# Two MoE blocks behind a sigmoid attention: the layers in pairs, and seven products in the second matrices of all batches

## Chip, core and metric

One core of one Trainium2 chip. The metric is the device time of one launch in microseconds (us), and lower is better.

## What is computed

Four batches of 448 tokens go through a sigmoid attention (12 heads of 64) and then through two blocks of 768 channels:

```python
x = attention(q, k, v)                      # 4 x 448 tokens, 768 channels, fp32
xn = x / rms(x) * rms_g                     # first block, inner width 1536
x = (silu(xn @ w_gate) * (xn @ w_val)) @ w_out
h = x @ w_in                                # second block, inner width 2048
out = (h - tanh(h)) @ w_out2
```

## The kernel before

Channels lie on the 128 partitions, and the 448 tokens of a batch are the columns of a matmul. An fp32 factor is split into a high part (rounded to fp32r) and a low part (the rest), and a product is three matmuls: high by high, high by low, low by high. So three matmuls of 448 columns make a "product" of one 128x128 weight block and one tile of tokens.

Two batches are worked on together: `BATCHES = ((0, 1), (2, 3))`. For a pair of batches a 2x2 block of weights times a 2x2 block of tokens takes eight products, or seven with sums of blocks in Strassen's manner (Winograd's form; `PRODUCTS` names the seven: A11 by B11, S1 by T1 and so on). The sums on the token side (T1 to T4) are made by VectorE in `right_sum`, those on the weight side (S1 to S4) likewise. Names: phase "A" is w_gate and w_val (`"Ag"`, `"Av"`), "B" is w_out, "C" is w_in of the second block, "D" is its w_out.

The work is a list `jobs`. A job of A or C is one pair of output chunks: seven times 3 products, 63 matmuls (`seven_units`, L934). A job of B or D takes four inner chunks into all six output chunks: as a SET with seven products 126 matmuls (`set_units`, L877), as PLAIN blocks with eight 144 (`block`, L959). Before, batches 0, 1 run through all of A, B, C, D first, with B and D in rows of six plain blocks; then batches 2, 3 do the same, with six SETs and one PLAIN set. Partial sums of B and D between groups go to DRAM and come back into PSUM by a copy (`seed`).

Weights arrive as float64 words (768 KB a row of six blocks) and are turned into fp32 by two instructions (`values32`, L350 and a cast). For batches 0, 1 this is done once, and the fp32 values, or for three pairs of C the split parts, are written to DRAM. Batches 2, 3 read them back: A and C by SyncE's queue into two buffers of kind `again`, B and D by GpSimd's queue, three jobs ahead (`fetch`), whence the sums S1 to S4 are made anew. Then each factor is split by a cast and a subtraction (L285, L361).

The order on each engine is not the order in the text. Every step is recorded with `add(engines, ...)` with an estimate of its duration, and `Plan.issue` lists the steps onto engines: it looks up to 500 steps ahead, picks by rank among those that can start soonest, and also chooses between ScalarE and VectorE where a copy or a cast may run on either. All DMAs but GpSimd's stand in one queue on SyncE (SP), in that order.

Buffers that the steps below touch: `xs`, 42 units, hold the seven split token factors of three chunk pairs (7 x 3 x 2), so that one pair of batches' factors of A or C fill them; `again` has two buffers; `raw` has three, after the change two.

Of the kernel before, what the change touches and what calls it, by code (L numbers as in the profile page):

```python
# [21 lines left out]
P = 128  # L22
# [3 lines left out]
GR = {"B": 6, "D": 4}  # L26
SG = 4
SPLIT = [("C", p) for p in range(3)]
# [10 lines left out]
FEED = 80  # L39
WINDOW = 500  # L40
N_UNIT, N_MOE, N_RAW, N_WT, N_CV = 74, 40, 3, 9, 3
BACK = 3
# [5 lines left out]
ORDER_1_OUT = [(k, m) for g in range(0, KF1, GR["B"]) for m in range(KM) for k in range(g, g + GR["B"])]  # L48
ORDER_2 = [(k, m) for m in range(KF2) for k in range(KM)]
ORDER_2_OUT = [(k, m) for g in range(0, KF2, GR["D"]) for m in range(KM) for k in range(g, g + GR["D"])]  # L50
# [168 lines left out]
def tile_sigmoid_attention_moe_moe(  # L219
# [81 lines left out]
    PLAIN_FROM = {"B": KF1 - SG, "D": KF2}  # L301
    PG = {ph: KM * n // NB for ph, n in GR.items()}
    PAIRS = {"Ag": (w_gate, "A"), "Av": (w_val, "A"), "C": (w_in2, "C")}
    SECOND = {"B": (w_out, ORDER_1_OUT), "D": (w_out2, ORDER_2_OUT)}


    for bs in BATCHES:
        for names, ph, n, ahead in (
            ([(ph, p) for p in range(KF1 // 2) for ph in ("Ag", "Av")], "B", KF1 // (SG if bs == BATCHES[1] else GR["B"]), int(bs == BATCHES[1])),
            ([("C", p) for p in range(KF2 // 2)], "D", KF2 // (SG if bs == BATCHES[1] else GR["D"]), 1),  # L310
        ):
            per, at = len(names) // n, 0
            for g in range(n):
                to = min((g + 1) * per + ahead, len(names))
                jobs += [(x, bs, p, None) for x, p in names[at:to]]
                if bs == BATCHES[1]:
                    jobs.append((ph, bs, g, SET if g * SG < PLAIN_FROM[ph] else PLAIN))
                else:
                    jobs += [(ph, bs, i, SECOND[ph][1][i * NB:(i + 1) * NB]) for i in range(g * PG[ph], (g + 1) * PG[ph])]
                at = to  # L320
    half = [j for j in range(len(jobs)) if jobs[j][1] == BATCHES[1]][0]


    raws, whls, got, ops = {}, {}, {}, {}
# [861 lines left out]
```

## Time and profile before

| what | us |
|---|---|
| median of 3 runs | 1094.83 (1094.33 to 1095.99) |
| the profiled execution | 1093.64 |
| its span, first to last instruction | 1091.5 |
| TensorE matmuls busy | 1073.5 |
| TensorE weight loads busy | 895.5 |
| VectorE busy | 766.8 |
| ScalarE busy | 574.6 |
| GpSimd busy | 59.6 |

An engine's busy time is the union of its instructions' spans. Matmuls are pipelined and one lasts longer (367 ns) than the step from one to the next, so the step is read from counts in a stretch. The profile is of one execution; the runs' median lies 1.2 us above it.

### The profile page before, as it was taken

How to read it: one execution, taken by the hardware profiler on the slowest of the kernel's cores; microseconds unless marked ns; L12 is line 12 of the kernel's file. 1: busy time of each engine (PE TensorE's matmuls, PEld its weight loads, DVE VectorE, ACT ScalarE, POOL GpSimd, SP SyncE). 2: the span in 40 equal slices, each digit the busy share in tenths (PEclk: the TensorE clock that was granted, in tenths of full speed). 3: DMA queues.
4: the chain of work that ended last, by engine and by line, in shares of the span. 5: the costliest groups of instructions: out<-in, count | busy, mean ns of one | idle time of the engine just before them, and what ended most of it. 6: DMA issues, size and time to landing. Idle time of an engine off the chain costs nothing. (4 is left out here: it accounts for less than half of the span.)

```text
span 1091.5 us, 14829 instructions
## 1 busy us (share of the span) xinstructions
PE 1073.5 (98%) x5256; PEld 895.5 (82%) x5256; DVE 766.8 (70%) x1217; ACT 574.6 (53%) x1036; POOL 59.6 (5%) x76
## 2 busy tenths in 40 slices
PE   9999999999999999999999999999999999999998
PEld 3333338999999998899998889999999889998997
DVE  0453816888488879878786887858855578786877
ACT  5776864552255556446464643444444556565652
POOL 0000000000000000000010000010040000113130
PEclk9999999999999999999999999999999999999999
DMA  5773553588748928699999654353495344538383
GB/s 167 255 218 112 143 180 129 203 260 283 226 162 281 330 112 313 203 315 309 313 345 317 226 185 121 113 200 102 107 224 187 118 147 140 192 86 189 57 207 126
DMA packets 115241, 215.73 MB, mean 198 GB/s; under 512 B 26720, under 2 KB 80992, under 8 KB 115168
## 3 DMA queue, kind: packets, MB, share of 16 engines
q1 hardware_dynamic: 106544, 195.36, 54.4%
q0 software_dynamic: 8320, 19.27, 8.0%
q8 instruction: 41, 0.67, 0.3%
q14 instruction: 32, 0.26, 0.1%
q10 hardware_dynamic: 304, 0.16, 0.0%
HBM read 135.71 MB, written 79.04 MB: 197 GB/s over the span
## 5 line engine op out<-in xcount | busy, mean ns | idle before, releaser
L934 PE MATMUL ps<-unit,wt 128*128 128x448 f32 x2520 | 523.4, 367 | 8.2 <-ACT unit L285 5.1
L934 PEld LDWEIGHTS ps<-unit,wt 128*128 128x128 f32 x2520 | 473.2, 188 | 53.1 <-ACT unit L285 8.4
L285 ACT COPY unit<-ps 128x448 f32<-128x448 f32 x220 | 115.9, 533 | 244.8 <-PE ps L934 91.9
L959 PE MATMUL ps<-unit,wt 128*128 128x448 f32 x1152 | 237.9, 366 | 1.8 <-ACT unit L285 1.8
L959 PEld LDWEIGHTS ps<-unit,wt 128*128 128x128 f32 x1152 | 216.2, 188 | 21.1 <-ACT unit L285 2.1
L361 DVE TENSOR_TENSOR wt<-cv,wt 128x768 fp32r<-128x768 f32 (+1 forms) x188 | 163.5, 876 | 20.9 <-ACT wt L285 17.8
L877 PE MATMUL ps<-unit,wt 128*128 128x448 f32 x756 | 158.0, 367 | 2.5 <-DVE unit L680 1.3
L877 PEld LDWEIGHTS ps<-unit,wt 128*128 128x128 f32 x756 | 141.3, 188 | 16.4 <-DVE unit L806 2.3
L285 ACT CAST wt<-cv 128x768 fp32r<-128x768 f32 (+1 forms) x136 | 104.5, 774 | 89.1 <-PE ps L934 40.4
L680 DVE TENSOR_TENSOR unit<-unit 128x448 fp32r<-128x448 f32 x168 | 102.4, 621 | 18.8 <-ACT unit L285 15.8
L285 ACT CAST unit<-unit 128x448 fp32r<-128x448 f32 x162 | 90.0, 567 | 35.1 <-DVE unit L789 14.4
L806 DVE TENSOR_TENSOR unit<-ps,unit 128x448 f32<-128x448 f32 x132 | 81.4, 621 | 28.3 <-PE ps L934 14.8
L582 ACT ACTIVATE unit<-ps 128x448 f32<-128x448 f32 (+1 forms) x192 | 86.4, 548 | 5.1 <-PE ps L575 5.1
L575 PE MATMUL ps<-wt 64*128 64x448 f32 (+1 forms) x384 | 78.9, 548 | 0.0
L605 PE MATMUL ps<-unit,vs 128*64 128x448 f32 (+1 forms) x384 | 77.7, 546 | 0.0
L350 DVE SCALAR_TENSOR_TENSOR cv<-wt,zero 128x768 uint32<-128x768 uint32 x68 | 64.8, 953 | 7.4 <-ACT zero L285 4.4
L575 PEld LDWEIGHTS ps<-wt 64*128 64x128 f32 (+1 forms) x384 | 32.3, 173 | 43.2 <-issue 36.2
L685 DVE TENSOR_TENSOR unit<-unit 128x448 f32<-128x448 f32 x96 | 59.1, 620 | 10.0 <-ACT unit L285 7.0
L605 PEld LDWEIGHTS ps<-unit,vs 128*64 128x64 f32 (+1 forms) x384 | 25.3, 136 | 49.0 <-issue 32.9
L285 ACT CAST zero<-wt 128x768 f16<-128x768 bf16 x48 | 51.8, 1079 | 20.3 <-DVE cv L350 13.2
L627 DVE TENSOR_TENSOR unit<-unit 128x448 f32<-128x448 f32 x20 | 12.5, 624 | 66.6 <-ACT unit L620 66.5
L419 DVE TENSOR_TENSOR cv<-cv 128x384 f32<-128x384 f32 x80 | 43.2, 554 | 19.2 <-DMA wC<-cv 10.8
(51 smaller groups left out, 523.2 us busy)
## 6 DMA issues: line engine op xcount, KB each, us to landing
wt<-in_w_out SPq DMA_DIRECT2D x28, 768.0 KB, 6.5
wt<-in_w_in SPq DMA_DIRECT2D x16, 768.0 KB, 6.9
sumD<-unit SPq DMA_DIRECT2D x48, 224.0 KB, 4.4
unit<-sumD SPq DMA_DIRECT2D x48, 224.0 KB, 5.3
wt<-in_w_gate SPq DMA_DIRECT2D x12, 768.0 KB, 5.4
wt<-in_w_val SPq DMA_DIRECT2D x12, 768.0 KB, 5.3
wAg<-cv SPq DMA_DIRECT2D x24, 384.0 KB, 4.6
wAv<-cv SPq DMA_DIRECT2D x24, 384.0 KB, 4.5
```

The source lines that it names most:

```text
L285: add(engines, lambda e: (nc.scalar.copy if e == "ACT" else nc.vector.tensor_copy)(to(), of()), reads, writes)
L350: add(dve(NW, psum=False), lambda e: nc.vector.scalar_tensor_tensor(out=c.tile.bitcast(U32), in0=r.tile[:, :NW, 1], scalar=13, in1=z.tile, ...
L361: add({**dve(n, psum=False), **pool(n)}, lambda e: ENG[e].tensor_sub(lo(), of(), hi().bitcast(F32)), [*reads, *kh], [*kl])
L575: nc.tensor.matmul(ps[i, c].tile[:n, :S], lhsT=t.tile[rows, at:at + n], rhs=t.tile[rows, :S], start=True, stop=True)
L582: add(act(S, psum=True), lambda e: nc.scalar.activation(to.tile[at:at + n, :S], ps.tile[:n, :S], AF.Sigmoid, bias=-math.log(S), scale=1.0 ...
L605: nc.tensor.matmul(ps.tile[i * D:(i + 1) * D, :S], lhsT=v.tile[:n, c, i, :], rhs=a[c][i].tile[:n, :], start=(c == 0), stop=(c == 3))
L680: add({**pool(S), **dve(S, psum=False)}, lambda e: ENG[e].tensor_sub(t["l"].tile, of.tile, t["h"].tile.bitcast(F32)), [of["t"], kh], [kl])
L685: add({**dve(S, psum=False), **pool(S)}, lambda e: ENG[e].tensor_sub(t.tile, x.tile, y.tile), [x["t"], y["t"]], [t["t"]])
L806: add(dve(S), lambda e: nc.vector.tensor_add(t.tile, ps.tile[:, :S], t.tile), [ps["t"], t["t"]], [t["t"]])
L877: nc.tensor.matmul(ps.tile[:, :S], lhsT=part(a), rhs=x[b].tile, start=n in (1, 5) and kp == 0 and q == 0, stop=kp == n_kp - 1 and q == 2, ...
L934: nc.tensor.matmul(ps.tile[:, :S], lhsT=part(a), rhs=x[b].tile, start=n in ((1, 2, 5) if opening else (1, 5)) and i == 0 and q == 0, stop= ...
L959: nc.tensor.matmul(ps.tile[:, :S], lhsT=wt, rhs=a[p].tile, start=start and i == 0, stop=stop and i == 2, skip_group_check=True)
```

## The change

Jobs are ordered by pairs of layers. A and B run for batches 0, 1, then for 2, 3; then C and D for batches 0, 1, then for 2, 3. B and D of batches 0, 1 use SETs too: both first B sets and all four D sets; the third B set is PLAIN for both pairs of batches. The rows of w_out and w_out2 are loaded, turned into fp32 and summed to S1 to S4 once, ahead of their use (`rows_early`): those of w_out beside the attention of batches 0 and 1, those of w_out2 beside A of batches 2, 3. All seven factors are written to DRAM. Every SET of every pair of batches reads its seven factors back one by one through SyncE's queue and the two `again` buffers (`again`). B's sums of all batches go to DRAM, by a write for the first set and an adding DMA on GpSimd's queue for the others, and C reads them back (`reload_sum`), with the token factors of C made beside the last job of the layer pair ahead. The three pairs of C whose split parts were stored store fp32 values now. In the two MoE blocks all copies and casts go to ScalarE.

```diff
-SPLIT = [("C", p) for p in range(3)]
+SPLIT = []
+ACT_COPIES = "AgAvBCD"
+PLAIN_SETS = {("B", 0): (2,), ("D", 0): (), ("B", 1): (2,), ("D", 1): ()}
...
-N_UNIT, N_MOE, N_RAW, N_WT, N_CV = 74, 40, 3, 9, 3
+N_UNIT, N_MOE, N_RAW, N_WT, N_CV = 74, 40, 2, 8, 5
...
-    for bs in BATCHES:
-        for names, ph, n, ahead in (
...
+    for names, ph in (
+        ([(x, p) for p in range(KF1 // 2) for x in ("Ag", "Av")], "B"),
+        ([("C", p) for p in range(KF2 // 2)], "D"),
+    ):
+        for bs in BATCHES:
...
+                jobs.append((ph, bs, g, PLAIN if is_plain(ph, bs, g) else SET))
...
+        return [lambda: get("A21", "A22"), lambda: of("A21"), lambda: of("A22"), lambda: total("S1", "A21", "A22", None, sub=False),
+                lambda: get("A11", "A12"), lambda: of("A11"), lambda: total("S3", "A11", "A21", "A21"),
+                lambda: total("S2", "S1", "A11", "S1"), lambda: of("A12"), lambda: total("S4", "A12", "S2", None)]
...
+    def again(d, at):
+        w = slot("again", cv_p, [P, NW], F32, "cv")
+        add({"SP": (1100, False)}, lambda e: nc.sync.dma_start(out=w.tile, in_=d.tile[:, at]), [d[at]], [w[0], w[1]], after=2500)
+        return w
...
+        def one(n):
+            w = again(whole_w[ph, i], ROWS.index(n))
+            whole((j, n), lambda: w.tile, [w[0], w[1]])
...
+    def reload_sum(b, c):
+        x = xg[b, c] = unit("xr")
+        d = sums_t.pop(("B", b, c))
+        add({"SP": (650, False)}, lambda e: nc.sync.dma_start(out=x.tile, in_=d.tile), [d["t"]], [x["t"]], after=2000)
...
-    PHASES = (1, 2, 5, 6, 7, 3, 4)
+    PHASES = {False: (1, 2, 5, 6, 3, 7, 4), True: (1, 5, 6, 3, 7, 2, 4)}
...
-    mixed(attn_units(0))
-    mixed(attn_units(1), [lambda: norm(0), lambda: spread_norm(0)])
+    rows_b = [u for i in range(n_sets("B")) for u in rows_early("B", i)]
+    mixed(attn_units(0), rows_b[:8])
+    mixed(attn_units(1), [lambda: norm(0), lambda: spread_norm(0)], rows_b[8:])
...
-        (last_c, half, [lambda: [spread_norm(b) for b in BATCHES[1]], *x_units(BATCHES[1], True)]),
+        (last["Av", BATCHES[0]], first["Ag", BATCHES[1]], [lambda: [spread_norm(b) for b in BATCHES[1]], *x_units("A", BATCHES[1], True)], BEHIND),
+        (last["Av", BATCHES[1]], first["C", BATCHES[0]], x_units("C", BATCHES[0], True), BEHIND),
+        (last["C", BATCHES[0]], first["C", BATCHES[1]], x_units("C", BATCHES[1], True), BEHIND),
+        (first["Ag", BATCHES[1]], first["C", BATCHES[0]] - 5, [u for i in range(n_sets("D")) for u in rows_early("D", i)], ROWS_BEHIND),
```

On TensorE, behind the attention, before: A of batches 0, 1 (L934) and the rows of w_out (L959), up to the start of C.

```order
L934 MATMUL ps<-unit,wt 128x448 x291
L959 MATMUL ps<-unit,wt 128x448 x6
L934 MATMUL ps<-unit,wt 128x448 x18
L959 MATMUL ps<-unit,wt 128x448 x210
L934 MATMUL ps<-unit,wt 128x448 x360
L959 MATMUL ps<-unit,wt 128x448 x6
L934 MATMUL ps<-unit,wt 128x448 x18
L959 MATMUL ps<-unit,wt 128x448 x210
```

The same place after: L937 are A's products, L880 those of a SET, L962 plain blocks, L661 the spread of the norm of batches 2, 3.

```order
L937 MATMUL ps<-unit,wt 128x448 x234
L880 MATMUL ps<-unit,wt 128x448 x9
L937 MATMUL ps<-unit,wt 128x448 x9
L880 MATMUL ps<-unit,wt 128x448 x108
L937 MATMUL ps<-unit,wt 128x448 x9
L880 MATMUL ps<-unit,wt 128x448 x9
L937 MATMUL ps<-unit,wt 128x448 x171
L962 MATMUL ps<-unit,wt 128x448 x24
L661 MATMUL ps<-unit,ones 128x448
L937 MATMUL ps<-unit,wt 128x448 x3
```

Two groups of 216 plain matmuls (6 and 210 in a row) have become two SETs of 126, of which the second is shown, and one PLAIN set of 144, whose first 24 stand at the end.

On SP, in the first third of the attention, before: loads of q, k (in_qkt) and v (in_vp), and between them the first weights of A.

```order
L536 DMA wt<-in_qkt 128x832
L541 DMA wt<-in_qkt 64x64 x2
L340 DMA wt<-in_w_gate 128x3072
L546 DMA vs<-in_vp 128x384
L546 DMA vs<-in_vp 32x128
L546 DMA vs<-in_vp 64x64 x2
L536 DMA wt<-in_qkt 128x832
L541 DMA wt<-in_qkt 64x64 x2
L340 DMA wt<-in_w_gate 128x3072
```

The same place after: the rows of w_out, and the first stores of their fp32 values (wB).

```order
L536 DMA wt<-in_qkt 128x832
L541 DMA wt<-in_qkt 64x64 x2
L336 DMA wt<-in_w_out 128x3072
L546 DMA vs<-in_vp 128x384
L546 DMA vs<-in_vp 32x128
L546 DMA vs<-in_vp 64x64 x2
L336 DMA wt<-in_w_out 128x3072
L536 DMA wt<-in_qkt 128x832
L541 DMA wt<-in_qkt 64x64 x2
L546 DMA vs<-in_vp 128x384
```

Up to the loads of attention pair 18 of 24 the queue held 5 weight loads and 9 stores of weights before; now it holds 12 loads and 18 stores.

On TensorE at the end of C and D of batches 0, 1, before: the last C job, the last group of rows of w_out2, then A of batches 2, 3.

```order
L934 MATMUL ps<-unit,wt 128x448 x6
L661 MATMUL ps<-unit,ones 128x448 x2
L934 MATMUL ps<-unit,wt 128x448 x39
L959 MATMUL ps<-unit,wt 128x448 x6
L934 MATMUL ps<-unit,wt 128x448 x18
L959 MATMUL ps<-unit,wt 128x448 x138
L934 MATMUL ps<-unit,wt 128x448 x297
```

The end of C and D of batches 0, 1 after: the last C job, the last D set, then C of batches 2, 3.

```order
L937 MATMUL ps<-unit,wt 128x448 x45
L880 MATMUL ps<-unit,wt 128x448 x9
L937 MATMUL ps<-unit,wt 128x448 x9
L880 MATMUL ps<-unit,wt 128x448 x108
L937 MATMUL ps<-unit,wt 128x448 x9
L880 MATMUL ps<-unit,wt 128x448 x9
L937 MATMUL ps<-unit,wt 128x448 x171
```

The 144 plain matmuls between the two layers have become 126, and what follows is another pair of batches in the same layer.

## Rows read from the trace of the kernel before

**Rows 1.** The page, engines' busy time, share of the span, instructions.
```profile
PE 1073.5 (98%) x5256; PEld 895.5 (82%) x5256; DVE 766.8 (70%) x1217; ACT 574.6 (53%) x1036; POOL 59.6 (5%) x76
```

**Rows 2.** Busy time by stretches: length, engines' us (x instructions), PEclk, DMA share, GB/s.
```profile
0.00:50.00 50.00, 48.06 (x236) 18.84 (x238) 10.96 (x16) 33.31 (x73) 1.60 (x8) 1.00 0.67 202
50.00:100.00 50.00, 50.00 (x256) 19.35 (x252) 21.01 (x37) 34.09 (x73) 1.04 (x1) 1.00 0.63 190
...
300.00:350.00 50.00, 50.00 (x247) 46.08 (x246) 41.82 (x66) 25.49 (x40) 0.00 (x0) 1.00 0.66 226
...
400.00:450.00 50.00, 46.74 (x226) 41.68 (x225) 43.76 (x72) 28.26 (x47) 0.00 (x0) 1.00 0.74 262
...
600.00:650.00 50.00, 47.05 (x219) 42.03 (x219) 42.75 (x75) 27.53 (x53) 0.00 (x0) 0.97 0.66 220
...
700.00:750.00 50.00, 50.00 (x248) 46.11 (x247) 34.66 (x52) 20.29 (x35) 3.03 (x4) 1.00 0.50 158
...
850.00:900.00 50.00, 46.68 (x226) 41.76 (x226) 33.93 (x56) 29.32 (x59) 1.51 (x2) 1.00 0.42 139
...
1050.00:1091.50 41.50, 36.62 (x178) 32.82 (x177) 28.01 (x44) 12.25 (x22) 0.91 (x2) 0.99 0.48 145
```

**Rows 3.** TensorE's waits over the whole span: us in total, times, longest.
```profile
PE ps L934 <- ACT unit L285: 5.1, 4, 2.2
PE ps L934 <- DVE unit L806: 2.6, 2, 1.3
PE ps L292 <- POOL mark L1030: 1.9, 1, 1.9
PE ps L959 <- ACT unit L285: 1.8, 1, 1.8
PE ps L877 <- DVE unit L680: 1.3, 1, 1.3
PE ps L877 <- DVE unit L806: 1.2, 1, 1.2
PE ps L934 <- ACT ps L285: 0.2, 1, 0.2
```

**Rows 4.** Groups by form: busy us, mean ns of one, idle before, releasers.
```profile
L934 PE MATMUL ps<-unit,wt 128*128 128x448 f32 x2520 | 523.4, 367 | 8.2 <-ACT unit L285 5.1 <-DVE unit L806 2.6 <-ACT ps L285 0.2
...
L361 DVE TENSOR_TENSOR wt<-cv,wt 128x768 fp32r<-128x768 f32 x151 | 143.6, 955 | 18.1 <-ACT wt L285 15.7
L680 DVE TENSOR_TENSOR unit<-unit 128x448 fp32r<-128x448 f32 x168 | 102.4, 621 | 18.8 <-ACT unit L285 15.8 <-DMA sumD<-unit 0.6
L285 ACT CAST wt<-cv 128x768 fp32r<-128x768 f32 x110 | 91.7, 835 | 78.0 <-PE ps L934 32.0 <-DVE cv L350 21.8 <-DVE cv L419 9.2
...
L350 DVE SCALAR_TENSOR_TENSOR cv<-wt,zero 128x768 uint32<-128x768 uint32 x68 | 64.8, 953 | 7.4 <-ACT zero L285 4.4 <-DMA wAg<-cv 1.4 <-DMA wC<-cv 0.8
L685 DVE TENSOR_TENSOR unit<-unit 128x448 f32<-128x448 f32 x96 | 59.1, 620 | 10.0 <-ACT unit L285 7.0 <-DMA sumD<-unit 2.4
...
L419 DVE TENSOR_TENSOR cv<-cv 128x384 f32<-128x384 f32 x80 | 43.2, 554 | 19.2 <-DMA wC<-cv 10.8 <-DMA wAg<-cv 7.3
...
L361 DVE TENSOR_TENSOR wt<-cv,wt 128x384 fp32r<-128x384 f32 x37 | 20.6, 556 | 2.7 <-ACT wt L285 2.1
```

**Rows 5.** Short stretches at the first and second seam (columns as in Rows 2).
```profile
435.00:440.00 5.00, 3.71 (x19) 3.09 (x18) 4.90 (x10) 1.96 (x5) 0.00 (x0) 1.00 1.04 341
...
605.00:610.00 5.00, 4.42 (x14) 3.97 (x15) 4.80 (x9) 5.00 (x11) 0.00 (x0) 0.66 1.05 381
```

**Rows 6.** TensorE in order of time: start, us, instructions, idle before and releaser.
```profile
605.58 5.50 PE L934 MATMUL ps<-unit,wt 128*128 128x448 f32 x18 [2.18 <-ACT unit L285]
```

**Rows 7.** DMA issues: count, KB each, median us to landing.
```profile
wt<-in_w_in SPq DMA_DIRECT2D x16, 768.0 KB, 6.9
...
cv<-wAg SPq DMA_DIRECT2D x24, 384.0 KB, 3.3
...
wt<-wD POOLq DMA_DIRECT2D x16, 384.0 KB, 6.0
```

More of the change, by code (lines that the diff above doesn't have):

```diff
@@ L499, in tile_sigmoid_attention_moe_moe @@
+    def set_factors(j):
+        ph, _, i, kind = jobs[j]
+        def one(n):
+            w = again(whole_w[ph, i], ROWS.index(n))
+            whole((j, n), lambda: w.tile, [w[0], w[1]])
+        names, n = (("A11", "A12", "A21", "A22"), 2) if kind == PLAIN else ([PRODUCTS[x][0] for x in PHASES[is_tight(j) > 0]], 4)
+        units = [lambda n=n: one(n) for n in names]
+        later[j] = units[n:]
+        return units[:n]
     later = {}
@@ L514, in again_units, with two @@
             return [lambda at=at, names=names: load_parts(at, names) for at, names in enumerate(FACTORS)]
-        g = got.pop(j)
-        def two(t, names):
+        def two(at, names):
+            t = again(stored[ph, i], at)
             of = lambda: t.tile
@@ L807, in plus, with chunks_of @@
         return t
-    n_sets = lambda ph: {"B": KF1, "D": KF2}[ph] // SG
-    PHASES = (1, 2, 5, 6, 7, 3, 4)
+    def chunks_of(j):
+        i = jobs[j][2]
+        return range(i * SG // 2, (i + 1) * SG // 2) if jobs[j][3] else ()
+    PHASES = {False: (1, 2, 5, 6, 3, 7, 4), True: (1, 5, 6, 3, 7, 2, 4)}
+    is_tight = lambda j: next((x for x in (1, 2) if jobs[j][3] and jobs[j - x][3] is None
+                               and jobs[j - x][1] == jobs[j][1] and jobs[j - x][2] in chunks_of(j)), 0)
     def set_units(j, tight):
         ph, bs, s, _ = jobs[j]
-        last = s == n_sets(ph) - 1
+        last = carried(ph, bs, s)
         n_kp = SG // 2
+        late = tight > 0
         banks, accs, f = {}, {}, {}
@@ L946, in seven_units @@
             order = [(n, i) for n in (1, 5, 6, 2) for i in range(3)]
[L947 removed]
+        order += [(n, i) for n in (3, 7, 4) for i in range(3)]
         return [lambda n=n, i=i: product(n, i) for n, i in order]
@@ L999, in job_units @@
             return plain_units(j)
-        def one(n, k, m):
-            w = whls[j]
-            first, last = k % GR[ph] == 0, k % GR[ph] == GR[ph] - 1
-            if first:
-                prologue(ph, bs, m, k // GR[ph])
-            block(bs, ph, k, m, w, n, first and k < GR[ph], last)
-            if last:
-                for b in bs:
-                    epilogue(ph, bs, b, m, k // GR[ph])
-        return [lambda n=n, k=k, m=m: one(n, k, m) for n, (k, m) in enumerate(blocks)]
     pairs = [(b, p) for b in range(B) for p in range(HP)]
@@ L1089, in tile_sigmoid_attention_moe_moe @@
     held = []
[L1090 to L1093 removed]
     for j in range(len(jobs)):
[L1096 to L1098 removed]
         ahead = conv(j + AHEAD) + [lambda: load(j + 2 * AHEAD)]
[L1100 removed]
+        plan.act_copies = jobs[j][0] in ACT_COPIES
         kind = kind_of(j)
[L1102 removed]
+        tight = is_tight(j)
         units = job_units(j, tight)
[L1104 to L1106 removed]
+        cut = {None: 3, SET: 3 if tight else 2, PLAIN: 4}[kind]
         order = units[:cut] + held + units[cut:]
         held = []
[L1109 to L1111 removed]
+        n = 2 if kind == PLAIN else HELD
+        order, held = order[:-n], order[-n:]
         for n, u in enumerate(order):
             u()
[L1114 removed]
+            for j0, j1, more, behind in beside:
                 if j0 <= j < j1:
```

302 lines of the change are left out of this document (128 added, 174 removed).

## The prediction, on record before the changed kernel ran

> **What bounds the kernel now.** I read the page's busy times first: TensorE has work for 98% of the span, VectorE for 70%, ScalarE for 53% [rows 1]. A busy TensorE need not be one at its best pace, so next comes the table by stretches. An undisturbed 50 us hold 247 or 248 matmuls [rows 2], which is 50 / 248 = 0.2016 us from one to the next; the 367 ns that one lasts [rows 4] is pipelined and no price. Three stretches hold fewer: 226, 219 and 226 [rows 2]. The list of TensorE's waits says why: 14.1 us in all, of which 1.9 is the start, the others on copies by ScalarE and additions by VectorE [rows 3]. Those three stretches are seams, where one layer's results become the next layer's token factors. Together they lack 22 + 29 + 22 = 73 matmuls, 73 x 0.2016 = 14.7 us. So the bound is the number of matmuls at 0.2016 us, plus what the seams lose, plus small waits inside the sets (1.3 and 1.2 us, L877 [rows 3]) and the end.
>
> At the first seam VectorE is the one that is late: busy 4.90 of 5 us while TensorE gets 19 matmuls instead of 25 [rows 5]. At the second there is a wait of 2.18 us, and the 18 matmuls behind it take 5.50 us [rows 6] instead of 18 x 0.2016 = 3.6; the granted clock of that stretch is 0.66 [rows 5], so a part of it ran at the lower of TensorE's two levels, 1.2 instead of 2.4 GHz. That wait cost its own length and 1.9 us more.
>
> **The matmuls.** Six groups of plain blocks (two of B, four of D, batches 0, 1, counted in sets of four inner chunks) become SETs: 144 - 126 = 18 matmuls fewer each, 108 in all. A, C, the attention and the third B set keep theirs. At 0.2016 us that is 21.8 us, and nothing hides it, since TensorE is what everything waits for. The Trainium skill ("TensorE: Matmul & The Clock Gate", section "Wait — 56ns, not 53.3ns?") puts a warm stream at columns / 2.4 GHz plus some 2.5 ns, an estimated 0.189 us for 448 columns; by that the term would be 20.4 us. The counts of this trace give 0.2016, with a weight load before each matmul, and they decide.
>
> **The seams.** Before, the last group of B had to be finished before C of the same batches could begin, and that of D before the units of batches 2, 3. Now each seam has another pair of batches in between, so the sums are long done and come back from DRAM; the DMAs (12 of 224 KB at each seam) are not late, as a whole set stands before them. What stays is the work to make the token factors. The `xs` buffers hold one layer's factors, so new ones start only as the last A or C job uses up the old ones. A seam needs 12 sums and 21 low parts on VectorE, 33 x 0.62 us [rows 4] = 20.5 us. At the start of C for batches 0, 1 there is also: two conversions of C pairs, each 2 x 0.953 + 4 x 0.554 + 3 x 0.955 + 0.556 = 7.5 us [rows 4], so 15.1; four splits of the PLAIN set, 3.8; and ten outputs of the last job at 0.62, 6.2. That is 45.6 us. Groups overlap a little at their ends, and the forms of the page add to 5% more than VectorE's 766.8 us, so I count 43.3. TensorE has 63 + 144 = 207 matmuls for it, 41.7 us. VectorE is thus full, not badly overfull. For the C(0, 1) to C(2, 3) seam the sum is 20.5 + 7 (conversions are reloads) + 8.7 (set) + 10.5 (last job's outputs and factors) = 46.7, some 44 against 189 x 0.2016 = 38.1, but a third of the new factors is wanted only inside the first job, 12.7 us later. The A seam is as the C(0, 1) one. A seam can cost nothing (the first products want only two of three chunk pairs) or as much as the worst of before, 29 x 0.2016 = 5.8 us; I take 2.3 each, 7 in all, nearer to the lower end as no chain through the last sums is left. Bounds 0 and 18. So the seams give back 14.7 - 7 = 7.7 us.
>
> **The sets.** Twelve SETs instead of six. The two waits inside sets came to 2.5 us for six, so 2.5 more for six further ones. Those of D for batches 0, 1 stand in the densest stretch: per two C jobs and one set (252 matmuls, 50.8 us) VectorE has two conversions 15.1, the outputs of the jobs 7.5, their token factors 22 x 0.62 = 13.6, seven splits 6.7 and six additions 3.7, together 46.6, by the same 5% 44.3 of 50.8, or 87%. Before, a stretch at 41.82 of 50 ran without a wait [rows 2], and one at 43.76 had the first seam. I add 1.5 us for that, so 4 in all; bounds 0 and 12. ScalarE takes over casts and copies: by the order's counts some 70 more casts of 768 columns at 835 ns [rows 4], 58 us, and about 140 more of 448 columns, estimated at two thirds of that, 80 us. That lifts it from 53% to some 66%. It stays behind VectorE, which rises by only some 20 us by the same counts, since it gives up most of its casts and copies.
>
> **The attention.** The queue takes 7 more weight loads and 9 more stores by pair 18, as the order shows: 7 x 0.786 + 9 x 0.393 = 9.0 MB. At 341 GB/s, which the queues reached at share 1.04 [rows 5], this is 26 us of full DMA within about 100 us, whose share was 0.67 and 0.63 [rows 2]. It becomes about 0.92: full, but the q, k, v loads stand up to three pairs (some 19 us) ahead. VectorE is free there, 10.96 and 21.01 us of 50 [rows 2], and takes most of the conversions. I take 1 us; bounds 0 and 8.
>
> **The sum**, against the profiled execution: 1093.64 - 21.8 - 7.7 + 4 + 1 = 1069.1. The runs' median lies 1.2 us above that execution, so 1070.3; I say 1070.
>
> **The rivals.**
> *Free seams*: 14.7 us come back whole, the sets cost 2.5. 1093.64 - 21.8 - 14.7 + 2.5 + 1.2 = 1060.8. For it speaks that the sums are ready a set ahead; against it the 43 us of VectorE in 42.
> *VectorE becomes the bound* in C and D of batches 0, 1 and at the seams: it decides when VectorE gets no more than the 42 of 50 us that it had in the fullest quiet stretch [rows 2]. Then 44.3 us per cycle take 52.7, 1.9 too many, four times 8; and the seams cost as before. 1093.64 - 21.8 + 8 + 4 + 1.2 = 1085.0. Against it: 4.90 of 5 was reached where it was pressed [rows 5].
> *The clock*: each seam leaves a wait like that of 2.18 us, with 1.9 us at the lower clock behind it, so 3 x 4.1 = 12 in place of 7: 1075. This lies inside the forecast's range. The Trainium skill ("TensorE: Matmul & The Clock Gate", section "What's actually happening") says that activity releases the throttle and idleness brings it back. The trace agrees in one place of seven, granted clock 0.66.
> *The reload loop* (slower): every SET's factor now passes through two `again` buffers: DMA, cast 0.835, subtraction 0.955 [rows 4]. TensorE uses one factor per 18 matmuls, 3.63 us. With the 3.3 us that such a load took [rows 7] a buffer turns in 5.1, and two give one factor every 2.55 us. At the 6.9 us of the w_in loads [rows 7] it is (6.9 + 1.79) / 2 = 4.35, 0.72 too slow, times 84 factors = 60 us: 1093.64 - 21.8 + 60 + 1.2 = 1133. It eats the gain from 6.0 us on, which is what the old set loads took on GpSimd's queue [rows 7]. Against it: A of batches 2, 3 made four such reloads per 12.7 us, one in 3.2 us, and held 248 matmuls per 50 us [rows 2].
> *The attention starves*: DMA full for 75 us, q and k come late by more than their lead. Price up to 10 us: 1080.
>
> **How the numbers follow.** Forecast 0.60 (1063 to 1079), free seams 0.17, VectorE 0.13, starved attention 0.05, reload loop 0.05. The range takes the free seams with some room, and VectorE as the bound: 1058 to 1087. About 0.2%, 2.2 us, is what a measurement of this kernel can tell from no change. Only the reload loop, and the tail of VectorE's case, end above 1092.6: faster 0.94, same 0.02, slower 0.04.
>
> **What would show it.** TensorE's three lines of products must count 2520, 1512 and 288, and an undisturbed 50 us must still hold 247 or 248. The seams should show waits of TensorE on VectorE or ScalarE of 1 to 3 us, the first 150 us none. If free seams are right, no stretch of 50 us falls below 240. If VectorE binds, it is over 45 of 50 us through D of batches 0, 1, with TensorE short in each of its four cycles. If the reload loop binds, ScalarE's casts in the sets wait for DMAs from the stored factors, and these land after 5 us or more. I am wrong in kind if the pace of matmuls changes, or if the three seams lose more than before.

## The result, and the profile after

The changed kernel takes 1102.44 us (median of 4 runs, 1100.51 to 1102.72) where the kernel before took 1094.58 beside it: a ratio of 1.0069, 95% interval 1.005 to 1.0087. It is slower by 0.7%; the forecast was 1070 us, in a range up to 1087. The profiled execution has a span of 1098.7 us (1091.5 before).

The page of the changed kernel, busy times, and the two large DMA queues (packets, MB, share of 16 engines' time):

```profile
PE 1058.4 (96%) x5148; PEld 878.0 (80%) x5148; DVE 770.1 (70%) x1207; ACT 706.7 (64%) x1268; POOL 99.9 (9%) x120
...
q1 hardware_dynamic: 92368, 215.02, 58.9%
q0 software_dynamic: 15552, 24.78, 14.1%
```

The same two queues in the kernel before:

```profile
q1 hardware_dynamic: 106544, 195.36, 54.4%
q0 software_dynamic: 8320, 19.27, 8.0%
```

TensorE has its 108 matmuls fewer than in [rows 1], and is busy for less of the span. Queue 0 is GpSimd's. After, it carries the adding DMAs (adds, for short) and nothing else: 108 of 224 KB are the 24.78 MB. Its share is 0.141 x 1098.7 = 155 us of all 16 engines, **1.43 us for each add**. Before there were 36 adds, and 28 loads of 384 KB.

The stretches that answer to [rows 2] (length, busy us and instructions of PE, PEld, DVE, ACT, POOL, granted clock, DMA share, GB/s):

```profile
50.00:100.00 50.00, 48.79 (x247) 18.93 (x249) 21.89 (x33) 36.35 (x79) 1.03 (x1) 1.00 0.89 291
...
300.00:350.00 50.00, 50.00 (x247) 46.05 (x246) 35.52 (x61) 31.52 (x54) 10.62 (x12) 1.00 0.84 217
...
400.00:450.00 50.00, 45.23 (x220) 40.88 (x220) 37.03 (x57) 28.00 (x49) 4.91 (x6) 1.00 0.86 255
...
600.00:650.00 50.00, 46.97 (x219) 41.99 (x220) 36.45 (x58) 29.66 (x52) 5.26 (x6) 0.97 0.54 157
...
700.00:750.00 50.00, 48.95 (x240) 44.50 (x239) 45.01 (x71) 39.95 (x68) 0.00 (x0) 1.00 0.78 266
750.00:800.00 50.00, 45.11 (x213) 41.11 (x211) 36.52 (x58) 31.55 (x56) 10.38 (x12) 0.94 0.75 194
800.00:850.00 50.00, 43.83 (x215) 40.19 (x213) 33.52 (x54) 29.44 (x55) 10.47 (x12) 0.98 0.67 170
850.00:900.00 50.00, 46.49 (x211) 41.33 (x212) 42.41 (x71) 36.00 (x69) 10.36 (x12) 0.95 0.79 200
...
1000.00:1050.00 50.00, 50.00 (x249) 46.29 (x248) 35.15 (x55) 32.97 (x60) 9.60 (x12) 1.00 0.70 167
```

A quiet stretch still holds 247 to 249 matmuls, so the pace is that of before. But more stretches are not quiet, above all the three from 750 to 900 us (D of batches 0, 1, and the seam behind it). In them GpSimd issues 12 adds each, and in the first two VectorE is far from full. In the last row shown, and in that from 300 us, there are 12 adds too and nothing is lost in the row itself: the adds alone are not enough. (Batches 2, 3, in the last row, convert no weights; that this is what spares them is not shown.)

A balance of the span needs the pace. A stretch counts the matmuls that are under way at its edges, so counts of short stretches are a little high; from start to start the step is 0.2033 us (650 to 850 us of the kernel before). By their starts, the first 200 us hold 970 matmuls (before 989), 3.9 us lost. From 200 us on the other 4178 should take 849.4 of 898.7 us, so 49.3 us are lost with the end; before, 4267 should take 867.5 of 891.5, so 24.0. Hence 1091.5 - 22.0 + 3.9 + 25.3 = 1098.7: the matmuls came off as counted, and 25 us more than before went in waits behind 200 us.

TensorE's two largest waits (in total, times, longest), against 5.1 and 2.6 us in [rows 3]:

```profile
PE ps L937 <- ACT unit L289: 12.2, 4, 6.3
PE ps L937 <- DVE unit L816: 10.0, 5, 4.9
```

The longest, in order of time (start, us, engine, line, and in brackets the idle time before and who ended it):

```profile
829.69 1.76 POOL L754 DMA_DIRECT2D out<-unit  x2 [1.01 <-DVE unit L816]
...
833.24 0.53 ACT L289 COPY unit<-ps 128x448 f32<-128x448 f32 x1 [4.65 <-DMA out<-unit]
...
840.69 0.32 SPq L677 DMA_DIRECT2D unit<-sumB  x1
...
848.81 0.83 ACT L289 CAST wt<-cv 128x768 fp32r<-128x768 f32 x1 [4.30 <-DMA cv<-wC]
...
850.13 6.20 PE L937 MATMUL ps<-unit,wt 128*128 128x448 f32 x18 [6.29 <-ACT unit L289]
```

The chain that led there (start, us, what):

```profile
829.69 8.79 DMA out<-unit
...
840.20 0.88 DVE wt L370
...
841.11 7.68 DMA cv<-wC
```

Read both upwards. TensorE waits 6.29 us for ScalarE, which stands at a cast whose fp32 weights (`cv<-wC`) come 7.7 us after their issue. That load was issued late: the buffer that it fills was in use until VectorE's subtraction (L370) ended at 841.08, and ahead of it in SP's queue the read of a sum (L677) stood until 840.69. VectorE was late itself, by the chain, because an add issued at 829.69 held a unit until it landed after 8.79 us; and ScalarE had stood still for 4.65 us already, for the same reason. Adds land after 8 us (DMA issues: count, KB, median us to landing):

```profile
sumB<-unit POOLq DMA_DIRECT2D x48, 224.0 KB, 8.4
out<-unit POOLq DMA_DIRECT2D x36, 224.0 KB, 8.0
...
cv<-wD SPq DMA_DIRECT2D x56, 384.0 KB, 3.9
```

In stretches of 5 us the DMA engines are full there, and the clock is low behind the wait:

```profile
840.00:845.00 5.00, 3.83 (x19) 3.21 (x18) 3.88 (x6) 2.10 (x4) 1.73 (x2) 1.00 1.11 244
845.00:850.00 5.00, 0.00 (x0) 0.00 (x0) 0.50 (x2) 1.19 (x3) 0.00 (x0) 0.83 1.11 281
850.00:855.00 5.00, 4.87 (x13) 4.35 (x14) 3.49 (x5) 3.97 (x8) 0.00 (x0) 0.50 0.95 355
```

A granted clock of 0.50 is the lower level, 1.2 GHz: 18 matmuls took 6.20 us instead of some 3.7 (18 x 0.2033).

Theory, then: **the 72 additional adds fill the DMA engines in dense stretches**, loads and stores come late, and the engines that work in order pass it on to TensorE. Rivals: the adds hurt by their landing time alone (held units); the reloads of all SET factors are what is too much; the seven products or the order cost it.

### The profile page after: what moved, and what is told of

Same layout as the page of the kernel before. It is cut to its first block, busy times and chain, and to the rows that moved or that the text cites. A ratio compares the mean times of both kernels' runs of the same rounds, so it can differ in the third digit from the quotient of the medians.

```text
span 1098.7 us, 15000 instructions
## 1 busy us (share of the span) xinstructions
PE 1058.4 (96%) x5148; PEld 878.0 (80%) x5148; DVE 770.1 (70%) x1207; ACT 706.7 (64%) x1268; POOL 99.9 (9%) x120
## 3 DMA queue, kind: packets, MB, share of 16 engines
q0 software_dynamic: 15552, 24.78, 14.1%
## 4 chain that ended last, share of the span: by engine, by line
PE 58%; issue 11%; DMA 8%; DVE 4%; ACT 2%; POOL 2%; POOLq 0%; SPq 0%; DVEq 0%; ACTq 0%
PE ps L937 35%; PE ps L880 20%; PE ps L962 3%; DMA out<-unit 1%; POOL out L754 1%; DVE wt L370 1%; DMA cv<-wB 1%; DMA cv<-wAv 1%; DMA unit<-sumB 1%; DMA wt<-in_w_out 1%; ACT wt L289 1%; DMA cv<-wC 1%; DVE unit L685 1%; DMA wt<-in_w_gate 1%; DVE unit L816 1%
## 5 line engine op out<-in xcount | busy, mean ns | idle before, releaser
L937 PE MATMUL ps<-unit,wt 128*128 128x448 f32 x2520 | 530.0, 369 | 22.9 <-ACT unit L289 12.2
L937 PEld LDWEIGHTS ps<-unit,wt 128*128 128x128 f32 x2520 | 476.9, 190 | 69.1 <-ACT unit L289 14.5
L880 PE MATMUL ps<-unit,wt 128*128 128x448 f32 x1512 | 316.3, 366 | 7.3 <-ACT wt L289 3.4
L880 PEld LDWEIGHTS ps<-unit,wt 128*128 128x128 f32 x1512 | 283.0, 188 | 35.0 <-ACT wt L289 4.8
L370 DVE TENSOR_TENSOR wt<-cv,wt 128x768 fp32r<-128x768 f32 (+1 forms) x252 | 223.0, 891 | 113.4 <-ACT wt L289 112.1
L289 ACT CAST wt<-cv 128x768 fp32r<-128x768 f32 (+1 forms) x248 | 193.4, 785 | 92.4 <-DVE cv L359 22.3
L289 ACT COPY unit<-ps 128x448 f32<-128x448 f32 x298 | 156.8, 533 | 116.8 <-PE ps L937 40.8
L685 DVE TENSOR_TENSOR unit<-unit 128x448 fp32r<-128x448 f32 x252 | 152.6, 620 | 28.5 <-ACT unit L289 22.1
L289 ACT CAST unit<-unit 128x448 fp32r<-128x448 f32 x258 | 142.1, 567 | 38.9 <-DVE unit L690 17.7
L816 DVE TENSOR_TENSOR unit<-ps,unit 128x448 f32<-128x448 f32 x168 | 103.8, 621 | 30.2 <-PE ps L937 14.6
L690 DVE TENSOR_TENSOR unit<-unit 128x448 f32<-128x448 f32 x144 | 87.5, 620 | 19.8 <-DMA unit<-sumB 16.4
L754 POOL DMA_DIRECT2D sumB<-unit x48 | 42.1, 990 | 438.5 <-DMA cv<-wB 157.1
L605 PEld LDWEIGHTS ps<-unit,vs 128*64 128x64 f32 (+1 forms) x384 | 25.3, 136 | 50.5 <-issue 32.1
L962 PE MATMUL ps<-unit,wt 128*128 128x448 f32 x288 | 61.1, 368 | 1.8 <-DVE unit L740 1.0
L962 PEld LDWEIGHTS ps<-unit,wt 128*128 128x128 f32 x288 | 53.5, 188 | 8.4 <-DVE unit L740 1.8
```

Source lines behind the costliest of these rows:

```text
L289: add(engines, lambda e: (nc.scalar.copy if e == "ACT" else nc.vector.tensor_copy)(to(), of()), reads, writes)
L370: add({**dve(n, psum=False), **pool(n)}, lambda e: ENG[e].tensor_sub(lo(), of(), hi().bitcast(F32)), [*reads, *kh], [*kl])
L605: nc.tensor.matmul(ps.tile[i * D:(i + 1) * D, :S], lhsT=v.tile[:n, c, i, :], rhs=a[c][i].tile[:n, :], start=(c == 0), stop=(c == 3))
L685: add({**pool(S), **dve(S, psum=False)}, lambda e: ENG[e].tensor_sub(t["l"].tile, of.tile, t["h"].tile.bitcast(F32)), [of["t"], kh], [kl])
L690: add({**dve(S, psum=False), **pool(S)}, lambda e: ENG[e].tensor_sub(t.tile, x.tile, y.tile), [x["t"], y["t"]], [t["t"]])
L816: add(dve(S), lambda e: nc.vector.tensor_add(t.tile, ps.tile[:, :S], t.tile), [ps["t"], t["t"]], [t["t"]])
```

## Experiments: which part of the change

**The order alone.** B and D of batches 0, 1 plain, all else as after.

```diff
-PLAIN_SETS = {("B", 0): (2,), ("D", 0): (), ...
+PLAIN_SETS = {("B", 0): (0, 1, 2), ("D", 0): (0, 1, 2, 3), ...
```

> The changed kernel with plain sets (eight products) in w_out and w_out2 of batches 0, 1; the new order of layers, the rows made ahead, the reloads and the adding DMAs stay. 108 matmuls more, 21.8 us at 0.2016 us. If what the changed kernel loses hangs on the seven products of batches 0, 1 (their token factors and seven reloads instead of four), the losses of 350 to 600 and 700 to 900 us mostly go, some 25 us, and the run ends near 1098. If it hangs on the new order, the sums through adding DMAs and the seams, the run ends at 1115 or more.

Measured 1115.86 us (ratio to before 1.0214, 1.0182 to 1.0245). The seven products are worth 1115.86 - 1102.44 = 13.4 us; order, reloads and adds without them cost 21. So most of the loss is not in the products; of the 22.0 us that 108 matmuls are worth, 8.6 did not come back under the adds.

**No additions in the DMAs.** The adds become plain writes.

```diff
-nc.gpsimd.dma_start(out=d.tile, in_=t.tile, accum_op=ALU.add)
+nc.gpsimd.dma_start(out=d.tile, in_=t.tile)
```

> The adding DMAs on GpSimd's queue become plain writes of the same tiles on the same queue; the additions are left out, so the sums hold only the last part. Theory of the adding DMAs (they land after 8 us, hold the units that ScalarE's next copies and SP's next loads need, and take the DMA engines from the others): 1075 to 1085, and ScalarE's waits on them in the D sets of batches 0, 1 are gone. Theory of the reloads (factors come late through two buffers) or of VectorE's load: within 5 us of the changed kernel's 1102.

Measured 1076.51 us (ratio 0.9851, 0.9829 to 0.9873): 25.9 us come back (24 by the ratios, as the kernel before was 1 us faster beside this run), and the time lies inside the forecast's range. Its queue 0, a row of its DMA issues, and the three stretches that had lost most (as above):

```profile
q0 software_dynamic: 6912, 24.78, 5.7%
...
out<-unit POOLq DMA_DIRECT2D x36, 224.0 KB, 3.0
...
750.00:800.00 50.00, 50.00 (x247) 46.06 (x246) 41.13 (x66) 35.81 (x63) 6.47 (x12) 1.00 0.57 200
800.00:850.00 50.00, 47.54 (x231) 42.59 (x230) 39.27 (x64) 36.20 (x67) 8.28 (x16) 1.00 0.72 242
850.00:900.00 50.00, 47.76 (x226) 43.20 (x225) 42.61 (x70) 33.45 (x62) 4.67 (x9) 0.97 0.46 145
```

The same bytes take 0.057 x 1073.2 / 108 = 0.57 us each instead of 1.43, and those of this row land after 3.0 instead of 8.0 us (those of B after 5.3 instead of 8.4).

**No reloads.** The factors of B and D are split from one fixed tile; 92 reloads of 384 KB are left out.

```diff
-            w = again(whole_w[ph, i], ROWS.index(n))
-            whole((j, n), lambda: w.tile, [w[0], w[1]])
+            whole((j, n), lambda: fixed, [])
```

> The factors of all sets of w_out and w_out2 are split from one fixed tile instead of being read back from DRAM: 92 loads of 384 KB are left out, the casts and subtractions stay. Theory of the reloads: 1075 to 1085, and casts no longer wait for these loads. Theory of the adding DMAs: 1095 or more, as ScalarE still stands behind results whose units are held.

Measured 1088.68 us (0.9954, 0.9939 to 0.9969): 13.8 us back. And both edits together:

> Plain writes for the adding DMAs and a fixed tile for the reloads of the sets together (additions and 92 loads left out). If the two costs are apart: 26 and 14 us off 1102, near 1063. If they are the same cost seen twice (a DMA system that is too full): 1072 to 1076, hardly below plain writes alone. Either way what is left over the number of matmuls is the work of VectorE and ScalarE at the seams and the attention.

Measured 1075.26 us (0.9838, 0.9823 to 0.9853), 1.2 us under the plain writes alone, with overlapping intervals. So the reloads cost nothing clear of the noise once the adds are light: 26 and 14 us do not add, as one common cause, a DMA system that is too full, would have it.

**A higher price in the planner.** Its estimate of an add's landing from 4000 to 7500 ns.

> Only the planner's estimate of when an adding DMA has landed changes, from 4.0 to 7.5 us behind its issue; the work is the same. Theory of the adding DMAs: the planner no longer puts copies and loads behind units that are still held, 1085 to 1095. Theory of the reloads: within 4 us of 1102.

Measured 1099.08 us (1.0067, 1.0042 to 1.0091): 3.4 us less than after at most, so the order of the work is not what is wrong, or not by that number.

**The attention.** The rows of w_out spread over the attention of three batches instead of two.

> The rows of w_out are spread over the attention of batches 0, 1 and 2 instead of 0 and 1; nothing else changes. If the attention loses its 3 to 4 us to a full DMA queue (share 0.89 from 50 to 100 us): 2 to 4 us faster than the changed kernel, and no wait of TensorE on loads of q and k or on sigmoids before 150 us. If it loses them to work that stands beside it on VectorE and ScalarE: no change or slower, since batch 2's attention already carries the token factors.

Measured 1104.9 us (1.0112, 1.0097 to 1.0127): the stretch from 50 us rose from 247 matmuls to 259, the next fell from 249 to 231. The loss moved with the work on the rows, to the stretch behind; the DMA share hardly changed (0.89 to 0.86 in the first of the two), so what makes it is not shown.

## Experiments: load or landing

**Units not held.** The adds take a fixed tile, so that no result unit waits for one; the sums are of that tile.

```diff
-lambda e: nc.gpsimd.dma_start(out=d.tile, in_=t.tile, accum_op=ALU.add), [t["t"], d["t"]], ...
+lambda e: nc.gpsimd.dma_start(out=d.tile, in_=fixed[:, :S], accum_op=ALU.add), [d["t"]], ...
```

> The adding DMAs stay on GpSimd's queue with their size, number and order, but each adds a fixed tile, so a result's unit is free as soon as it is written and does not wait for the DMA; the sums are left wrong by that. If the adding DMAs cost by holding the units that the next copies need: near the 1077 of the run with plain writes, and ScalarE no longer waits on them. If they cost by the time they take on the 16 DMA engines (14% of it against 6% for plain writes), and by that make stores, reloads and the read-back of sums late: 1092 or more.

Measured 1137.24 us (1.0414, 1.0395 to 1.0433). Freed of the results, the planner put the adds into bursts; the worst stretch:

```profile
750.00:800.00 50.00, 38.48 (x160) 33.73 (x159) 28.05 (x46) 23.67 (x42) 22.42 (x26) 0.86 1.10 289
```

26 adds in 50 us, DMA full, 160 matmuls. Held units are not needed for a loss. The bursts make it no clean test of how much they add, so another was made.

**The same load without adding.** Each add becomes two and a half plain writes, the further ones to scratch.

```diff
-            add({"POOL": ...}, lambda e: nc.gpsimd.dma_start(out=d.tile, in_=t.tile, accum_op=ALU.add), ...
+            add({"POOL": ...}, lambda e: nc.gpsimd.dma_start(out=d.tile, in_=t.tile), ...
+            for i, n in enumerate((S, S // 2)):
+                x = Slot(None, ...)
+                add({"POOL": ...}, lambda e, x=x, n=n: nc.gpsimd.dma_start(out=x.tile[:, :n], in_=t.tile[:, :n]), ...
```

> AFTER with each of the 108 adding DMAs replaced by two and a half plain writes on the same queue: one to the sum's place, one of the same size and one of half the size to scratch places (the additions are left out; the result unit is held until all three have landed). A plain write took 0.57 us of all 16 DMA engines and an add 1.43, so the load on the DMA engines is that of the adds, while no DMA reads and adds in place. Theory A, the load is what costs: 1096 to 1106, queue 0 again at some 14% of the engines' time. Theory B, an add costs by its own long landing (8 us against 3), by which units are held and readers wait, whatever it loads: the single writes land in 3 to 4 us, and 1077 to 1085.

Measured 1102.83 us (1.0079, 1.0049 to 1.0109), after's own time, with queue 0 at after's share and a landing of 4.9 us:

```profile
q0 software_dynamic: 19008, 61.95, 14.4%
...
out<-unit POOLq DMA_DIRECT2D x36, 224.0 KB, 4.9
...
350.00:400.00 50.00, 44.54 (x208) 39.43 (x207) 39.12 (x66) 29.14 (x51) 7.89 (x15) 0.97 0.87 308
400.00:450.00 50.00, 43.57 (x194) 37.45 (x193) 35.46 (x54) 25.67 (x45) 12.95 (x25) 0.93 0.95 342
...
850.00:900.00 50.00, 44.47 (x204) 38.98 (x204) 41.17 (x69) 34.72 (x67) 22.87 (x43) 0.97 0.88 319
```

ScalarE's waits on such DMAs (us in total, times, longest), in after, and then all that is left of them in this run:

```profile
ACT unit L289 <- DMA out<-unit: 6.9, 3, 4.6
ACT unit L289 <- DMA sumD<-unit: 3.0, 2, 1.9
```

```profile
ACT unit L289 <- DMA scr_B<-unit: 1.4, 1, 1.4
```

Plain writes that fill the engines as long as the adds cost as much in sum, though ScalarE waits 1.4 us for their landing and not 9.9. That speaks for the load. It is no proof that after's loss is load alone. A unit is held here until its three writes have landed, 6.4 us from the first issue in the median (an add 8.2, the plain write of the second experiment 4.0). And the loss is spread otherwise: 402 matmuls from 350 to 450 us (after 454), 678 from 750 to 900 (after 639). How after's 25.9 us divide between full engines and held units stays open.

The Trainium skill ("SBUF — State Buffer", section "Who interferes with whom") says of a DMA that seems stalled by a VectorE operation that it is one of GpSimd's, whose descriptors wait for a port that the two engines share. The runs speak against that as the cause here: the plain writes of the second experiment came from the same queue, with VectorE as busy (769.3 us against 770.1), and landed in 2.9 to 5.3 us (medians of the three sums).

**Adds where there is room.** The 36 adds of the kernel *before* become plain writes.

> The kernel BEFORE with its 36 adding DMAs turned into plain writes of the same 224 KB on the same queue (the additions to the sums are left out, nothing else). Density theory: 36 adds spread over the whole run, with whole pairs of sets between them, hide behind a DMA share of 0.6 to 0.8, so nothing is gained: 1091 to 1095, ratio 0.997 to 1.002. Rival, a fixed price for each add: after lost 26 us to 108 adds, 0.24 us each, so before loses 36 x 0.24 = 8.7 us: 1085, ratio 0.992.

Measured 1094.02 us (0.9998, 0.9985 to 1.0011): nothing.

```profile
q0 software_dynamic: 5440, 19.27, 5.0%
```

Its queue 0 falls from 8.0% to 5.0%, (87.3 - 54.6) / 36 = 0.91 us for each, near the 0.86 of the prices above (1.43 - 0.57); the time does not move.

**Stretch by stretch.** In after, only the 36 adds of D for batches 0, 1 become plain writes, or only the 48 of B.

> AFTER with only the 36 adding DMAs of the second layer, batches 0, 1, turned into plain writes (those additions are left out), and no read-backs or merges. The other 72 adds stay. If the load stands with its stretch, what after lost at 650 to 900 us comes back and nothing else changes: with 13 us of the 26, 1087 to 1092. If the adds cost only together, by the mean load, a third: 1093 to 1095. If nothing: the merges of e13 were not what cost, 1101 to 1104.

> AFTER with only the 48 adding DMAs of the first layer turned into plain writes (those additions are left out); the 60 of the second stay. The losses of after between 350 and 650 us were some 60 matmuls, 12 us, against 32 matmuls in e2_write: so some 6 to 12 us come back if each stretch pays for its own adds: 1090 to 1096. By count alone 48 of 108 of 26 us: 1091. The gains of this run and of e14_late should add up to the 26 us of e2_write if the stretches are independent; to more if half the adds would have been free.

Measured 1089.52 us (0.9958, 0.9938 to 0.9978) and 1090.65 us (0.9966, 0.9952 to 0.998), so 12.9 and 11.8 us, together 24.7 of the 25.9. That leaves 1 us, within the noise, for the other 24 (D of batches 2, 3). The first run's stretches from 400 and 750 us, then the second run's (columns as above):

```profile
400.00:450.00 50.00, 47.17 (x224) 42.83 (x223) 38.49 (x60) 29.22 (x52) 5.26 (x6) 0.97 0.89 262
...
750.00:800.00 50.00, 50.00 (x248) 46.03 (x246) 42.06 (x67) 36.61 (x65) 6.53 (x12) 1.00 0.58 206
```

```profile
400.00:450.00 50.00, 47.76 (x233) 43.16 (x232) 40.49 (x62) 30.53 (x53) 2.15 (x4) 1.00 0.74 253
...
750.00:800.00 50.00, 44.99 (x212) 41.11 (x212) 35.61 (x57) 30.45 (x54) 10.29 (x12) 0.93 0.73 181
```

Each stretch pays for its own adds: the DMA share falls, and the matmuls come back, where they were taken out. From 750 to 900 us the first run holds 66 matmuls more than after and the second 1; from 350 to 650 us it is 12 and 47.

## Experiments: sums in another way

All of these have complete sums. None beats the kernel before.

**Carried sums.** No adds: partial sums are read back by SP and added by VectorE, or seeded into PSUM, in every set (`carried` returns `s > 0`; buffers `accs` 6 instead of 9).

> No adding DMA at all, and the whole computation kept: from a group's second set on the sum so far is read back by SP's queue and added by VectorE as the products leave PSUM (as the last D set does already), or seeded into PSUM for the plain sets, and is written anew. 84 adding DMAs less, 84 more writes and 84 more reads on SP's queue, some 12 more additions of 0.62 us on VectorE per set and 12 fewer copies on ScalarE. Theory of the adding DMAs: 1076 to 1084. Theory of VectorE as the bound in D of batches 0, 1: its bill there rises by 7.4 us per 50.8 us cycle to about all of it, so 1088 or more, with VectorE above 47 of 50 us there.

(The adds are 108, not the 84 that stand there.) Measured 1105.09 us (1.0105, 1.0072 to 1.0138). The 108 further reads and 108 further writes lift the main queue, and VectorE gets additions (811.9 us busy in place of 770.1); the seam behind D of batches 0, 1:

```profile
q1 hardware_dynamic: 123472, 264.58, 71.0%
...
850.00:900.00 50.00, 40.58 (x166) 34.40 (x165) 43.75 (x74) 25.97 (x48) 0.00 (x0) 0.90 0.62 213
```

**GpSimd adds.** SP reads the partial sum, GpSimd adds, and writes it plainly.

> AFTER with each adding DMA replaced by a read of the partial sum into SBUF on SP's queue, an addition on GpSimd (91% idle), and a plain write on GpSimd's queue. Complete sums. The load on the DMA engines falls from 1.43 us for each to 2 x 0.57 = 1.14 or a little more. Theory A (load costs): a fifth of the 26 us comes back at most, 1095 to 1103. Theory B (the landing of the add costs): the write lands in 3 to 5 us, most of it comes back, 1079 to 1086, if GpSimd's addition takes no more than some 1.5 us. Third possibility: GpSimd's additions hold up VectorE, whose groups get longer by more than 3%, and it is slower than after, above 1105.

Measured 1130.49 us (1.0337, 1.0317 to 1.0356): the third possibility. Two groups of VectorE in after, then the same two and GpSimd's own in this kernel (count, busy us, mean ns):

```profile
L370 DVE TENSOR_TENSOR wt<-cv,wt 128x768 fp32r<-128x768 f32 x212 | 201.7, 954 | 103.3 <-ACT wt L289 102.2
L685 DVE TENSOR_TENSOR unit<-unit 128x448 fp32r<-128x448 f32 x252 | 152.6, 620 | 28.5 <-ACT unit L289 22.1 <-PE ps L880 3.8 <-DMA sumD<-unit 0.8
```

```profile
L370 DVE TENSOR_TENSOR wt<-cv,wt 128x768 fp32r<-128x768 f32 x212 | 223.6, 1058 | 83.3 <-ACT wt L289 81.8
L685 DVE TENSOR_TENSOR unit<-unit 128x448 fp32r<-128x448 f32 x252 | 178.7, 728 | 25.4 <-ACT unit L289 17.1 <-PE ps L883 3.7 <-POOL unit L756 3.3
...
L756 POOL TENSOR_TENSOR unit<-unit 128x448 f32<-128x448 f32 x108 | 132.1, 1228 | 693.9 <-DVE unit L819 461.3 <-PE ps L883 144.1 <-ACT unit L289 86.8
```

VectorE's subtractions of two SBUF tiles became 11% and 17% longer in the mean, 840.0 us busy in place of 770.1, so GpSimd's 91% of idle time was not free. The overlap is what does it: of the 212 of L370, the 172 that met no addition of GpSimd's took 955 ns as before, the 40 that met one 1501. The Trainium skill ("SBUF — State Buffer", section "Who interferes with whom") says just that: a VectorE instruction with two SBUF inputs contends with a GpSimd instruction that reads SBUF. The trace agrees.

**Merging later.** The sets of batches 0, 1 write their partial sums apart; one pair of batches later they are read, added by VectorE and written. First 60 adds so, through SP; then the same through GpSimd's queue and earlier; then only the 36 of D, through GpSimd's queue or through SP's.

```diff
-        if s:
+        if s and bs == BATCHES[0]:
+            d = sums_t[ph, b, m, s] = Slot(None, ...)      # a place of its own, plain write
...
+    def merge(ph, b, m):
+        d, a = sums_t[ph, b, m], unit("acc")
+        add({"SP": ...}, ... a.tile, in_=d.tile ...)
+        for s in range(1, n_sets(ph)):
+            x, y = sums_t.pop((ph, b, m, s)), unit("acc")
+            add({"SP": ...}, ... y.tile, in_=x.tile ...)
+            add(dve(S, psum=False), ... tensor_add(a.tile, a.tile, y.tile) ...)
+        add({"SP": ...}, ... d.tile, in_=a.tile ...)
```

> AFTER, complete sums, with the 60 adding DMAs of batches 0, 1 gone: each set's partial sum goes to a place of its own by a plain write, and one pair of batches later (from 450 us on for the first layer, from 900 us on for the second, where the DMA share was 0.5 to 0.7) SP reads the partial sums back, VectorE adds them (60 x 0.62 = 37 us, where it had 26 to 41 of 50 us to do) and SP writes the total. The 48 adds of batches 2, 3 stay. More bytes than after in all: 84 reads and 24 writes more, 60 x (1.43 - 0.57) = 52 us of DMA less in the dense stretches, 108 x 0.57 = 62 us more in the others. If the loss hangs on where the DMA load stands, as the share theory has it, most of the 26 us comes back: 1079 to 1088, below the kernel before. Rival, total load counts wherever it stands: 1100 to 1107, as after. Third, the in-order SP queue or VectorE becomes late in the new places: dips between 450 and 600 us and behind 900 us, 1090 to 1100.

> As e11_merge, with the read-backs and the totals of the merges on GpSimd's queue instead of SP's, and the merges earlier: those of the first layer within some 80 us behind 430 us, those of the second within some 130 us behind 890 us. Complete sums. If SP's order made e11 lose (a store of a total waits for VectorE and holds the loads behind it), the dips behind 550 and 1000 us go and 750 to 900 us keeps 225 to 247 matmuls for each 50 us: 1078 to 1090. If it was the DMA load that stood there (share 1.04 and 1.08), dips of the same size come where the merges stand now: 1100 to 1110.

> Only the 36 adding DMAs of the second layer, batches 0, 1, replaced by partial writes and late merges on GpSimd's queue, early behind 890 us, where after had a DMA share of 0.5 to 0.7 and no losses; the other 72 adds as in after. Complete sums. By the windows of after, 650 to 900 us lost some 110 matmuls or 22 us; e11 had 43 matmuls lost there. So 1102 - 13 = 1089 if the merges cost nothing behind 900 us; 1100 and more if the load makes the same loss wherever it stands.

> As e13_d, but read-backs and totals on SP's queue. If SP's order costs something by itself, this is slower than e13_d by 4 to 10 us; if only the load counts, the two agree within 3 us.

Measured 1108.42 us (1.0144, 1.0116 to 1.0172), 1112.33 (1.0173, 1.0148 to 1.0198), 1104.68 (1.0111, 1.008 to 1.0143) and 1103.78 (1.01, 1.0066 to 1.0133). The last two agree, so SP's order is not it. Stretches of the first of the four:

```profile
550.00:600.00 50.00, 41.78 (x193) 36.81 (x191) 27.24 (x41) 25.16 (x42) 10.34 (x12) 0.94 1.04 309
...
750.00:800.00 50.00, 50.00 (x247) 45.91 (x246) 41.80 (x65) 36.84 (x65) 6.55 (x12) 1.00 0.64 225
...
1000.00:1050.00 50.00, 42.86 (x202) 38.81 (x201) 35.03 (x56) 28.73 (x51) 4.80 (x6) 0.93 0.69 214
```

The dense stretch is whole again, and the losses stand where the merges went, once at a DMA share of 1.04. The clearest number: the same 36 adds taken away without merges gave 1089.52 us, with merges 1103.78, so 12 x 5 DMAs and 36 additions cost 14.3 us in a stretch that had lost nothing under 12 adds. There the share is 0.69 to 0.74, averaged over 50 us, and which of their DMAs or additions comes too late is not shown.

## Why the prediction was wrong

**The step that failed** is the list of what the change adds. "The DMAs (12 of 224 KB at each seam) are not late" prices the reading of the sums; the 72 further adds that write them stand in no term. They were in the change (every set but the first), and a bound was in the page of before: 87.3 us of queue 0 for 36 adds and 28 loads. The plain writes put the missing term at 25.9 us, of the 32 between 1070 and 1102; by the stretches, 12.9 of it belong to D and 11.8 to B.

**The matmuls**, -21.8: counts 2520, 1512 and 288 as forecast, and quiet stretches hold 247 to 249 as before. Right. The step of 0.2016 us was read a little short, since [rows 2] count a matmul under way at an edge in both stretches; at 0.2033 the term is 22.0. What the products gave in net, under the same adds, was 13.4.

**Seams and sets**, -7.7 and +4: under after's adds the two cannot be told from them. With plain writes the time from 200 us on holds 4171 matmuls, 848.0 of 873.2 us, so 25.2 lost against 24.0 before: +1.2 in place of -3.7. Mis-sized by 4.9 us, by the rows of that kernel mostly at the seams: 226 matmuls behind D of batches 0, 1, as many as at two of the old seams [rows 2]. "Free seams" is wrong.

**The attention**, +1: 3.9 lost in after, and with plain writes 977 matmuls in 200 us against 989, 2.4 us. The DMA share was forecast as 0.92 over about 100 us; it was 0.65 and 0.89 in the first two stretches. In size inside the bounds, though there were three waits of 0.4 to 1.3 us in the first 150 us, where none was forecast.

**The rivals.** VectorE did not bind: 36.52 and 33.52 of 50 us where most was lost. (From 700 to 750 us it is at 45.01 with 240 matmuls, but with plain writes at 44.83 with 239, so that is not what the adds cost.) The reload loop did not either: such loads landed in 3.9 to 4.6 us, under the 6.0 from which it decides, and leaving them out gains 1.2 us once the adds are light; only late loads in the full stretches, as the one of 7.7 us, did harm. The clock fell behind long waits as that rival had it, but the waits came from elsewhere. The attention did not starve. The condition that I named for being wrong in kind, seams that lose more than before, is what came. The slower side had the wrong mechanism and 4%.

## What to carry to other kernels

Price every DMA that a change adds, by kind and by the stretch it falls into, not only those that someone visibly waits for: a share of 0.67 in 50 us (from 800 us) hid 10 us at 1.11 here, where in-order engines pass each late load on. An accumulating DMA is to be counted at its own time on the DMA engines, here two and a half times a plain write. To find such a cost, replace the DMA by a plain one, then load the engines as much without the suspected operation; and note that shifting work to an idle engine or a quieter stretch returned nothing here, three times over.

## What the hardware showed

- An accumulating DMA of 224 KB from SBUF to DRAM took 1.43 us of all 16 engines, the plain write 0.57; it landed after 7.6 to 8.4 us against 2.9 to 5.3 (medians of the three sums). Plain writes of two and a half times the bytes took the same time of the engines (14.4% against 14.1%) and gave the same kernel time.
- With adds the DMA engines are full at less: share 1.11 at 244 to 288 GB/s from 835 to 850 us, around the long stall, where the plain writes' kernel moved 323 to 360 GB/s at 0.95 to 0.98 in the stretches that answer to them (810 to 830 us).
- GpSimd issued an add in 0.86 us in the median (1.76 for two, above) and a plain write in 0.54.
- Beside additions on GpSimd (128x448, 1228 ns), VectorE's subtractions of two SBUF tiles of 128x768 took 1501 ns where the two overlapped and 955 where not.
- TensorE behind a wait of 6.29 us was granted 0.50 of its clock, and 18 matmuls took 6.20 us.
